# Ordering small TensorE products by tile size, and moving a block's transposes from TensorE to the DMA crossbar

## The chip, the cores and the metric

The kernel runs on one core of one Trainium2 chip. The metric is the device time of one execution in microseconds (us), median over several runs. A run counts as slow when it is over 1.5% above the fastest run of the same kernel; the medians given here for the runs use the fast runs only. The granted clock is the share of its full speed that TensorE was allowed (1.00 is full); landing is the time from a DMA's issue to the arrival of its data; a transpose on the DMA crossbar is a DMA that transposes the tile that it moves. A ratio below is the mean time of one kernel's fast runs over that of the other's in the same rounds, so it is not quite the ratio of the medians that stand beside it.

## The reference, cut to what matters

```python
# 4 batches, 8 heads, 768 steps, head size 48
for t in range(S):                      # gated linear attention
    state = alpha[:, :, t, :, None] * state + einsum('bhd,bhe->bhde', k[:, :, t], v[:, :, t])
    y[:, :, t] = einsum('bhd,bhde->bhe', q[:, :, t], state)
x = y.transpose(0, 2, 1, 3).reshape(3072, 384)
r = maximum(x @ w_in, 0.0)              # w_in 384 x 2048
out = (s * r * r + b) @ w_out           # w_out 2048 x 384
```

## The kernel before

Attention works on 24 blocks of 128 steps (6 in each of 4 sequences), all 8 heads at once. For a block, b is the running product of alpha. The block needs the transposes of q\*b and k/b (4 tiles of 128x128 each), the score products, and the y products (state times q, and v times masked scores). The y products of 8 heads of 48 columns are cut at the borders of quadrants (32 columns each), so some are 64 columns wide and some 32.

```python
def st_T(n):                            # 8 transposes on TensorE, into PSUM
    for x, src in ((0, qb_sb[n % 2]), (1, kb_sb[n % 2])):
        f = src.rearrange("a h d -> a (h d)")
        for p in range(NP):
            nc.tensor.transpose(out=t_ps[:, x, p, :], in_=f[:, 128*p : 128*p + 128], identity=ident_bf)

def st_Tcopy(n):                        # VectorE copies them to SBUF
    nc.vector.tensor_copy(out=qkT_sb[n % 2]..., in_=t_ps...)

# (pair of heads, [head,] first 32-column quadrant, width in quadrants)
S_PARTS = [(0, 0, 2), (0, 2, 1), (1, 3, 1), (1, 4, 2), (2, 6, 2), (2, 8, 1), (3, 9, 1), (3, 10, 2)]
V_PARTS = [
    (0, 0, 0, 2), (0, 1, 2, 1), (1, 0, 3, 1), (1, 1, 4, 2), (2, 0, 6, 2), (2, 1, 8, 1),
    (3, 0, 9, 1), (3, 1, 10, 2), (0, 1, 1, 1), (1, 0, 4, 1), (2, 1, 7, 1), (3, 0, 10, 1),
]
def st_y(n):
    for p, x, m in S_PARTS: ...         # state^T q, 8 products
    for p, e, x, m in V_PARTS: ...      # v^T masked scores, 12 products
```

All work goes through a small list scheduler inside the kernel: each operation is booked with an engine, an assumed duration, a priority and a latency, the scheduler simulates, and the instructions are emitted in the order of its simulated start times. Each engine then runs its own list strictly in that order.

```python
op("SP", 0.98, rank + 0.1 * x, load, n, src, dst, w=[(name, ii)], lat=2.0)
op("PE", 0.5, t + 0.3, st_T, n, r=[("qb", i2), ("kb", i2)], w=["ct"], lat=0.27)
op("DVE", 0.61, t + 0.4, st_Tcopy, n, r=["ct"], w=[("qkT", i2)])
op("PE", 0.33, t + 0.5, st_A, n, r=[("qkT", i2)], w=["a"], lat=0.27)      # scores
op("PE", 0.6, t + 0.7, st_y, n, r=rr, w=["py"], lat=0.27)
op("ACT", 0.43, t + 0.8, st_yevac, n, r=["py"], w=[("xd", ...)])
# ... and the MLP: mm1 (w_in, PE), relu (ACT), square (DVE), mm2 (w_out, PE), output
```

## Time and profile before

| | before |
|---|---|
| median | 233.87 us (3 runs, 233.66 to 234.86; the profiled run took 235.56) |
| TensorE busy | 211.7 us of 233.8 |
| TensorE idle from 52 us to its last matmul | 0 |
| y products of one block | 1.70 us |

The windows view of the kernel before gives stretches of the run: from and to, length, then the busy time of TensorE, its weight loads, VectorE, ScalarE and GpSimd, the granted clock of TensorE, the mean busy share of the 16 DMA engines and their GB/s:

```profile
30.00:40.00 10.00, 8.06 (x86) 5.64 (x84) 7.20 (x13) 3.25 (x6) 7.21 (x5) 1.00 0.95 289
40.00:52.00 12.00, 10.33 (x95) 6.53 (x92) 12.00 (x21) 5.50 (x12) 4.39 (x4) 0.86 1.01 223
52.00:75.00 23.00, 23.00 (x240) 14.95 (x238) 18.72 (x44) 12.90 (x31) 5.16 (x7) 1.00 0.77 160
75.00:100.00 25.00, 25.00 (x276) 16.59 (x276) 16.08 (x41) 11.97 (x26) 4.49 (x7) 1.00 0.88 181
100.00:125.00 25.00, 25.00 (x242) 13.75 (x242) 17.29 (x32) 12.33 (x29) 3.32 (x5) 1.00 0.85 176
```

The first busy column is TensorE: it fills every stretch from 52 us on, so there each microsecond taken off it counts. Before 52 us it does not fill them. The DMA share is 0.77 to 0.88 from 52 to 125 us.

The first four groups of weight loads of one block's y products, in the timeline of TensorE's weight loads (start, duration, engine, line, operation, operands, array tile, count):

```profile
118.63 0.11 PEld L409 LDWEIGHTS <-s_st_144 128*64 128x64 bf16 x1 [0.42 <-issue]
118.80 0.10 PEld L409 LDWEIGHTS <-s_st_144 128*32 128x32 bf16 x2
118.97 0.11 PEld L409 LDWEIGHTS <-s_st_144 128*64 128x64 bf16 x2
119.14 0.10 PEld L409 LDWEIGHTS <-s_st_144 128*32 128x32 bf16 x2
```

A change between 128\*64 and 128\*32 tiles comes every 0.17 us, with one product in the group or two; the last group, at 120.16, has four and takes 0.17 us as well. Ten groups make the 1.70 us, which the chain of waits of the same block shows as two halves (start, duration):

```profile
118.70 0.85 PE py_ps L409 x8
119.55 0.85 PE py_ps L419 x12
120.40 0.76 PE o_ps_69 L479 x4
```

### The profile page before, as it was taken

How to read it: one execution, taken by the hardware profiler on the slowest of the kernel's cores; microseconds unless marked ns; L12 is line 12 of the kernel's file. 1: busy time of each engine (PE TensorE's matmuls, PEld its weight loads, DVE VectorE, ACT ScalarE, POOL GpSimd, SP SyncE). 2: the span in 40 equal slices, each digit the busy share in tenths (PEclk: the TensorE clock that was granted, in tenths of full speed). 3: DMA queues.
4: the chain of work that ended last, by engine and by line, in shares of the span. 5: the costliest groups of instructions: out<-in, count | busy, mean ns of one | idle time of the engine just before them, and what ended most of it. 6: DMA issues, size and time to landing. Idle time of an engine off the chain costs nothing.

```text
span 233.8 us, 4929 instructions
## 1 busy us (share of the span) xinstructions
PE 211.7 (91%) x1916; PEld 123.9 (53%) x1916; DVE 144.0 (62%) x283; ACT 100.8 (43%) x217; POOL 45.4 (19%) x63
## 2 busy tenths in 40 slices
PE   0268696799999999999999999999999999999993
PEld 0134473466676666655555555545555555555562
DVE  2266459998779666675767865597656754343321
ACT  3213351554565534523656545675354433444300
POOL 5234439333102220200202120001210100000000
PEclk9999999799999999999999999999999999999999
DMA  6999798995789989689895464300000100101111
GB/s 135 184 289 249 199 366 197 242 205 111 157 171 213 192 190 185 143 172 215 170 181 101 97 146 104 67 3 34 35 3 34 36 0 34 36 35 38 64 70 67
DMA packets 107320, 30.21 MB, mean 129 GB/s; under 512 B 100640, under 2 KB 105760, under 8 KB 107296
## 3 DMA queue, kind: packets, MB, share of 16 engines
q1 hardware_dynamic: 107296, 29.89, 55.2%
q8 instruction: 15, 0.25, 0.5%
q14 instruction: 9, 0.07, 0.1%
HBM read 25.17 MB, written 4.72 MB: 128 GB/s over the span
## 4 chain that ended last, share of the span: by engine, by line
PE 82%; SPq 7%; DVE 5%; DMA 3%; issue 1%; ACT 0%
PE h_ps_67 L455 14%; PE o_ps_69 L479 14%; PE h_ps_66 L455 14%; PE o_ps_68 L479 13%; PE py_ps L419 8%; PE py_ps L409 7%; SPq L175 5%; PE ct_ps L324 4%; PE a_ps L370 3%; PE py_ps L335 3%; DMA a_in_73<-in_alpha_dram 3%; PE ct_ps L281 2%; SPq L220 1%; DVE colpart L247 1%; DVE colsum L252 1%
## 5 line engine op out<-in xcount | busy, mean ns | idle before, releaser
L464 ACT ACTIVATE r_149<-h_ps_66 128x512 bf16<-128x512 f32 x48 | 28.7, 598 | 46.2 <-PE h_ps_66 L455 37.4
L455 PEld LDWEIGHTS <-w_in_bf 128*128 128x128 bf16 x384 | 34.9, 100 | 22.0 <-issue 2.1
L464 ACT ACTIVATE r_150<-h_ps_67 128x512 bf16<-128x512 f32 x48 | 28.7, 599 | 20.1 <-PE h_ps_67 L455 13.5
L455 PE MATMUL h_ps_66<-xd_147,w_in_bf 128*128 128x512 bf16 (+1 forms) x72 | 17.0, 357 | 0.0
L379 DVE TENSOR_TENSOR am_138<-a_ps,mask 128x1024 bf16<-128x1024 f32 x12 | 14.7, 1222 | 3.4 <-PE a_ps L370 3.2
L344 DVE COPY qkT_136<-ct_ps 128x1024 bf16<-128x1024 bf16 x12 | 8.3, 688 | 13.7 <-PE ct_ps L324 13.7
L455 PE MATMUL h_ps_67<-xd_147,w_in_bf 128*128 128x512 bf16 (+1 forms) x72 | 16.5, 348 | 0.0
L344 DVE COPY qkT_137<-ct_ps 128x1024 bf16<-128x1024 bf16 x12 | 8.3, 690 | 12.9 <-PE ct_ps L324 12.8
L379 DVE TENSOR_TENSOR am_139<-a_ps,mask 128x1024 bf16<-128x1024 f32 x12 | 14.7, 1221 | 2.3 <-PE a_ps L370 2.0
L455 PE MATMUL h_ps_67<-xd_146,w_in_bf 128*128 128x256 bf16 (+1 forms) x72 | 13.8, 321 | 1.5 <-ACT r_150 L464 1.5
L455 PE MATMUL h_ps_66<-xd_146,w_in_bf 128*128 128x256 bf16 (+1 forms) x72 | 13.9, 323 | 0.0
L364 POOL TENSOR_TENSOR s_st_144<-t_142,blast_140 128x384 bf16<-128x384 bf16 x8 | 7.7, 968 | 24.6 <-DVE t_142 L356 17.7
L433 ACT ACTIVATE xd_147<-py_ps 128x384 bf16<-128x384 f32 x10 | 4.9, 490 | 15.2 <-PE py_ps L419 15.2
L409 PE MATMUL py_ps<-qkT_137,s_st_144 128*64 128x128 bf16 (+1 forms) x96 | 11.4, 242 | 0.0
L324 PE MATMUL ct_ps<-ident_bf,qb_128 128*128 128x128 bf16 x48 | 5.1, 234 | 5.4 <-DVE qb_128 L308 5.4
L409 PEld LDWEIGHTS <-s_st_144 128*64 128x64 bf16 (+1 forms) x96 | 6.2, 101 | 6.9 <-issue 3.5
L455 PE MATMUL h_ps_66<-xd_148,w_in_bf 128*128 128x256 bf16 (+1 forms) x48 | 9.8, 327 | 0.0
L455 PE MATMUL h_ps_67<-xd_148,w_in_bf 128*128 128x256 bf16 (+1 forms) x48 | 9.8, 327 | 0.0
L364 POOL TENSOR_TENSOR s_st_145<-t_143,blast_141 128x384 bf16<-128x384 bf16 x8 | 7.0, 879 | 13.3 <-DVE t_143 L356 11.2
L419 PEld LDWEIGHTS <-vp_113 128*32 128x32 bf16 (+1 forms) x96 | 5.0, 99 | 6.3 <-issue 3.5
L281 PE MATMUL ct_ps<-la_97,U_bf 128*128 128x384 bf16 x12 | 4.5, 376 | 4.1 <-ACT la_97 L275 4.1
L295 ACT ACTIVATE b_s_125<-ct_ps 128x384 f32<-128x384 f32 x12 | 5.9, 489 | 5.4 <-PE ct_ps L286 5.1
(207 smaller groups left out, 480.8 us busy)
## 6 DMA issues: line engine op xcount, KB each, us to landing
out_dram<-o_sb_167 SPq DMA_DIRECT2D x8, 192.0 KB, 2.0
out_dram<-o_sb_168 SPq DMA_DIRECT2D x8, 192.0 KB, 2.0
out_dram<-o_sb_169 SPq DMA_DIRECT2D x8, 192.0 KB, 1.9
a_in_70<-in_alpha_dram SPq DMA_DIRECT2D x5, 192.0 KB, 4.2
q_in_75<-in_q_dram SPq DMA_DIRECT2D x5, 192.0 KB, 3.6
k_in_80<-in_k_dram SPq DMA_DIRECT2D x5, 192.0 KB, 3.9
v_in_85<-in_v_dram SPq DMA_DIRECT2D x5, 192.0 KB, 4.0
a_in_71<-in_alpha_dram SPq DMA_DIRECT2D x5, 192.0 KB, 3.6
```

Of the source, the lines that this page charges most:

```text
L175: nc.sync.dma_start(out=dst[n % NIN], in_=src[b, :, c * C : (c + 1) * C, :].rearrange("h s d -> s h d"),)
L281: nc.tensor.matmul(out=cum_ps, lhsT=U_bf, rhs=la[:, :, 0:D], start=True, stop=True)
L324: nc.tensor.transpose(out=t_ps[:, x, p, :], in_=f[:, 128 * p : 128 * p + 128], identity=ident_bf,)
L335: nc.tensor.matmul(out=p_ps[64 * e : 64 * e + 64, p, :], lhsT=kb[:, 128 * p + 64 * e : 128 * p + 64 * e + 64], rhs=vp[:, p, 48 * e : 48 * ...
L344: nc.vector.tensor_copy(out=qkT_sb[n % 2].rearrange("a x p t -> a (x p t)"), in_=t_ps.rearrange("a x p t -> a (x p t)"),)
L364: nc.gpsimd.tensor_tensor(out=s_sb[n % 2], in0=t1_sb[n % 2], in1=bl, op=ALU.mult)
L379: nc.vector.tensor_tensor(out=am_sb[n % 2].rearrange("a e p t -> a (e p) t"), in0=a_ps.rearrange("a e p t -> a (e p) t"), in1=mask.unsquee ...
L409: nc.tensor.matmul(out=y_ps[r0 : r0 + 32 * m, kk, :], lhsT=st[:, p, c0 : c0 + 32 * m], rhs=qT[:, p, :], start=(x < 4), stop=False,)
L419: nc.tensor.matmul(out=y_ps[r0 : r0 + 32 * m, kk, :], lhsT=vp[:, p, c0 : c0 + 32 * m], rhs=am[:, e, p, :], start=(first and i < 3), stop=( ...
L455: nc.tensor.matmul(out=hp[:, i * n : (i + 1) * n], lhsT=w_in_bf[:, kk, 128 * j : 128 * (j + 1)], rhs=xd_sb[g % 3][:, kk, 0:n], start=(kk = ...
L464: nc.scalar.activation(out=r_sb[w % 2], in_=h_ps[w % 2], func=AF.Relu)
L479: nc.tensor.matmul(out=op[:, 0:d_model], lhsT=gt_sb[j][:, c0 : c0 + C], rhs=w_out_bf[:, j, :], start=(j == 0), stop=(j == NJ - 1),)
```

## The change

The intent is to take work off TensorE in two ways: order the y products so that the tile size changes once, and give the transposes of blocks 4 to 23 to the DMA crossbar (one DMA of 128x1024 bf16 a block, issued by ScalarE), which also frees VectorE of its copy. To make room, q\*b and k/b share one tile with three buffers, and v has four buffers. Two loads of 128 x 1 elements (s and b) move from the SP queue to GpSimd.

```diff
+NPE = 4
-    vp_sb = many("vp", 3, ...)
+    vp_sb = many("vp", 4, ...)
-    qb_sb = many("qb", 2, [128, H, 64], BF16, zero=nc.vector)
-    kb_sb = many("kb", 2, [128, H, 64], BF16, zero=nc.vector)
-    qkT_sb = many("qkT", 2, [128, 2, NP, 128], BF16)
+    qk_sb = many("qk", 3, [128, 2, H, 64], BF16, zero=nc.vector)
+    qkT_sb = many("qkT", 3, [128, 2, NP, 128], BF16)
+    def st_Tdma(n):
+        nc.scalar.dma_start_transpose(
+            out=qkT_sb[n % 3].rearrange("a x p t -> a (x p) t"),
+            in_=qk_sb[n % 3].rearrange("a x h d -> a (x h d)"),
+        )
-    S_PARTS = [...]
-    V_PARTS = [...]
+    Y_PARTS = [                                     # None: a state product
+        (0, None, 0, 2), (2, None, 6, 2), (1, None, 4, 2), (3, None, 10, 2),
+        (0, 0, 0, 2), (2, 0, 6, 2), (1, 1, 4, 2), (3, 1, 10, 2),
+        (2, None, 8, 1), (3, None, 9, 1), (0, None, 2, 1), (1, None, 3, 1),
+        (2, 1, 8, 1), (3, 0, 9, 1), (0, 1, 2, 1), (1, 0, 3, 1),
+        (1, 0, 4, 1), (0, 1, 1, 1), (3, 0, 10, 1), (2, 1, 7, 1),
+    ]
     # ... st_y runs through Y_PARTS in this order
-                op("SP", 0.5, t + 0.5, lambda: nc.sync.dma_start(out=b_col, ...
+                op("POOL", 0.5, t + 0.5, lambda: nc.gpsimd.dma_start(out=b_col, ...
     # ... the same for s_col
+            if n < NPE:
                 op("PE", 0.5, t + 0.3, st_T, n, ...)
                 op("DVE", 0.61, t + 0.4, st_Tcopy, n, ...)
+            else:
+                op("ACT", 0.3, t + 0.3, st_Tdma, n, r=[("qb", i3), ("kb", i3)],
+                   w=[("qkT", i3)], lat=3.5)
-            op("PE", 0.6, t + 0.7, st_y, ...)
+            op("PE", 0.55, t + 0.7, st_y, ...)
```

More of the change, by code (lines that the diff above doesn't have):

```diff
@@ L192 @@
     nc.vector.memset(ones_col_bf, 1.0)
-    vp_sb = many("vp", 3, [128, NP, VW], BF16, zero=nc.gpsimd)
+    vp_sb = many("vp", 4, [128, NP, VW], BF16, zero=nc.gpsimd)
     mask = sb.tile([128, 128], BF16, name="mask")
@@ L302, in st_vcast @@
         nc.gpsimd.tensor_copy(
-            out=vp_sb[n % 3].rearrange("a p (x d) -> a p x d", d=D)[:, :, 0:3:2, :],
+            out=vp_sb[n % 4].rearrange("a p (x d) -> a p x d", d=D)[:, :, 0:3:2, :],
             in_=v_in[n % NIN].rearrange("a (p e) d -> a p e d", e=2),
@@ L308, in st_qb @@
         nc.vector.tensor_tensor(
-            out=qb_sb[n % 2][:, :, 0:D], in0=q_in[n % NIN], in1=b_sb[n % 2], op=ALU.mult
+            out=qk_sb[n % 3][:, 0, :, 0:D], in0=q_in[n % NIN], in1=b_sb[n % 2], op=ALU.mult
         )
@@ L313, in st_kb @@
         nc.vector.tensor_tensor(
-            out=kb_sb[n % 2][:, :, 0:D],
+            out=qk_sb[n % 3][:, 1, :, 0:D],
             in0=k_in[n % NIN],
@@ L320, in st_T @@
     def st_T(n):
-        for x, src in ((0, qb_sb[n % 2]), (1, kb_sb[n % 2])):
-            f = src.rearrange("a h d -> a (h d)")
+        f = qk_sb[n % 3].rearrange("a x h d -> a (x h d)")
+        for x in range(2):
             for p in range(NP):
+                c0 = 512 * x + 128 * p
                 nc.tensor.transpose(
-                    out=t_ps[:, x, p, :],
-                    in_=f[:, 128 * p : 128 * p + 128],
-                    identity=ident_bf,
-                )
+                    out=t_ps[:, x, p, :], in_=f[:, c0 : c0 + 128], identity=ident_bf
+                )
+    def st_Tdma(n):
[3 more added lines that the diff above has]
+        )
     def st_KV(n):
-        kb = kb_sb[n % 2].rearrange("a h d -> a (h d)")
-        vp = vp_sb[n % 3]
+        kb = qk_sb[n % 3][:, 1].rearrange("a h d -> a (h d)")
+        vp = vp_sb[n % 4]
         for p in range(NP):
@@ L344, in st_Tcopy @@
         nc.vector.tensor_copy(
-            out=qkT_sb[n % 2].rearrange("a x p t -> a (x p t)"),
+            out=qkT_sb[n % 3].rearrange("a x p t -> a (x p t)"),
             in_=t_ps.rearrange("a x p t -> a (x p t)"),
@@ L366, in st_A @@
     def st_A(n):
-        qkT = qkT_sb[n % 2]
+        qkT = qkT_sb[n % 3]
         for p in range(NP):
@@ L384, in st_mask @@
         )
-    def quadrant(x):
-        return x // 4, 32 * (x % 4)
-    S_PARTS = [(0, 0, 2), (0, 2, 1), (1, 3, 1), (1, 4, 2), (2, 6, 2), (2, 8, 1), (3, 9, 1), (3, 10, 2)]
-    V_PARTS = [
-        (0, 0, 0, 2), (0, 1, 2, 1), (1, 0, 3, 1), (1, 1, 4, 2), (2, 0, 6, 2), (2, 1, 8, 1),
-        (3, 0, 9, 1), (3, 1, 10, 2), (0, 1, 1, 1), (1, 0, 4, 1), (2, 1, 7, 1), (3, 0, 10, 1),
+    Y_PARTS = [
[5 rows of a table added]
     ]
@@ L400, in st_y @@
         first = n % NCH == 0
-        qT = qkT_sb[n % 2][:, 0]
+        qT = qkT_sb[n % 3][:, 0]
         am = am_sb[n % 2]
-        vp = vp_sb[n % 3]
+        vp = vp_sb[n % 4]
         st = s_sb[(n - 1) % 2]
-        if not first:
-            for p, x, m in S_PARTS:
-                kk, r0 = quadrant(x)
-                c0 = 32 * x - 96 * p
-                nc.tensor.matmul(
-                    out=y_ps[r0 : r0 + 32 * m, kk, :],
-                    lhsT=st[:, p, c0 : c0 + 32 * m],
-                    rhs=qT[:, p, :],
-                    start=(x < 4),
-                    stop=False,
-                )
-        for i, (p, e, x, m) in enumerate(V_PARTS):
-            kk, r0 = quadrant(x)
-            c0 = 32 * x - 96 * p + 48 * e
-            nc.tensor.matmul(
-                out=y_ps[r0 : r0 + 32 * m, kk, :],
-                lhsT=vp[:, p, c0 : c0 + 32 * m],
-                rhs=am[:, e, p, :],
-                start=(first and i < 3),
-                stop=(i >= 8),
+        parts = [x for x in Y_PARTS if not (first and x[1] is None)]
+        fresh = {0, 1, 2, 3}
+        for i, (p, e, x, m) in enumerate(parts):
+            c0 = 32 * x - 96 * p
+            mine = {(x + y) % 4 for y in range(m)}
+            start = mine <= fresh
+            fresh -= mine
+            nc.tensor.matmul(
+                out=y_ps[32 * (x % 4) : 32 * (x % 4) + 32 * m, x // 4, :],
+                lhsT=(
+                    st[:, p, c0 : c0 + 32 * m]
+                    if e is None
+                    else vp[:, p, c0 + 48 * e : c0 + 48 * e + 32 * m]
+                ),
+                rhs=qT[:, p, :] if e is None else am[:, e, p, :],
+                start=start,
+                stop=(i >= len(parts) - 4),
             )
@@ L527 @@
                     sched.done((name, 0), 3.5 + x)
-                op("SP", 0.5, t + 0.5,
-                   lambda: nc.sync.dma_start(out=b_col, in_=moe_b.to_broadcast((128, 1))),
+                op("POOL", 0.5, t + 0.5,
+                   lambda: nc.gpsimd.dma_start(out=b_col, in_=moe_b.to_broadcast((128, 1))),
                    w=["b"], lat=2.0)
-                op("SP", 0.5, t + 0.6,
-                   lambda: nc.sync.dma_start(out=s_col, in_=moe_s.to_broadcast((128, 1))),
+                op("POOL", 0.5, t + 0.6,
+                   lambda: nc.gpsimd.dma_start(out=s_col, in_=moe_s.to_broadcast((128, 1))),
                    w=["s"], lat=2.0)
@@ L567 @@
             op("ACT", 0.55, t + 0.1, st_exp_i, n, r=["ct"], w=[("bi", i2), ("bl", i2)])
-            op("POOL", 0.6, t + 0.2, st_vcast, n, r=[("v", ii)], w=[("vp", i3)])
-            op("DVE", 0.47, t + 0.2, st_qb, n, r=[("q", ii), ("b", i2)], w=[("qb", i2)])
-            op("DVE", 0.47, t + 0.2, st_kb, n, r=[("k", ii), ("bi", i2)], w=[("kb", i2)])
-            op("PE", 0.5, t + 0.3, st_T, n, r=[("qb", i2), ("kb", i2)], w=["ct"], lat=0.27)
-            op("DVE", 0.61, t + 0.4, st_Tcopy, n, r=["ct"], w=[("qkT", i2)])
-            op("PE", 0.34, t + 0.35, st_KV, n, r=[("kb", i2), ("vp", i3)], w=["py"], lat=0.27)
+            op("POOL", 0.6, t + 0.2, st_vcast, n, r=[("v", ii)], w=[("vp", n % 4)])
+            op("DVE", 0.47, t + 0.2, st_qb, n, r=[("q", ii), ("b", i2)], w=[("qb", i3)])
+            op("DVE", 0.47, t + 0.2, st_kb, n, r=[("k", ii), ("bi", i2)], w=[("kb", i3)])
+            if n < NPE:
+                op("PE", 0.5, t + 0.3, st_T, n, r=[("qb", i3), ("kb", i3)], w=["ct"], lat=0.27)
+                op("DVE", 0.61, t + 0.4, st_Tcopy, n, r=["ct"], w=[("qkT", i3)])
+            else:
+                op("ACT", 0.3, t + 0.3, st_Tdma, n, r=[("qb", i3), ("kb", i3)],
+                   w=[("qkT", i3)], lat=3.5)
+            op("PE", 0.34, t + 0.35, st_KV, n, r=[("kb", i3), ("vp", n % 4)], w=["py"], lat=0.27)
             if first(n):
@@ L578 @@
                 op("POOL", 0.9, t + 0.1, st_snew, n, r=[("t1", i2), ("bl", i2)], w=[("S", i2)])
-            op("PE", 0.33, t + 0.5, st_A, n, r=[("qkT", i2)], w=["a"], lat=0.27)
+            op("PE", 0.33, t + 0.5, st_A, n, r=[("qkT", i3)], w=["a"], lat=0.27)
             op("DVE", 1.15, t + 0.6, st_mask, n, r=["a"], w=[("am", i2)])
-            rr = [("am", i2), ("qkT", i2), ("vp", i3)] + ([] if first(n) else [("S", 1 - i2)])
-            op("PE", 0.6, t + 0.7, st_y, n, r=rr, w=["py"], lat=0.27)
+            rr = [("am", i2), ("qkT", i3), ("vp", n % 4)] + ([] if first(n) else [("S", 1 - i2)])
+            op("PE", 0.55, t + 0.7, st_y, n, r=rr, w=["py"], lat=0.27)
             op("ACT", 0.43, t + 0.8, st_yevac, n, r=["py"], w=[("xd", g % 3, blk_group[n][1])])
```

## The prediction

> **What bounds the kernel now.** The windows view has TensorE busy 23.00 of 23, 25.00 of 25, 25.00 of 25 ... in every stretch from 52 to 197 us, and the chain of waits is 82% TensorE. Before 52 us it is starved (0.57 of the first 10 us, 6 to 8 of each later 10): there the DMA share is 0.78 to 1.01 and VectorE is full from 40 to 52 us. After 197 us only MLP matmuls remain. From 52 to 197 us VectorE (99 of 145 us) and ScalarE (73) have slack. So this middle stretch, with attention blocks 4 to 23 at 7.2 us each, is where TensorE work removed counts one for one.
>
> **y products.** In the timeline of one block (118.6 to 120.3 us), the 20 products start in groups: 118.63 (64 columns), 118.80 (32, 32), 118.97 (64, 64), 119.14, 119.31, 119.48 ... 120.33. A change between 64 and 32 columns costs 0.17 us whether one, two or four products stand in the group: 10 groups = 1.70 us. This fits the Trainium skill, "TensorEngine Tiling (Array Packing)", Key Properties: changing the tiling mode drains the array, and tiles of one mode run in parallel. The k-v products, all 64 wide, show the second half: pairs at 114.29, 114.32, 114.36, 114.41 us, so two column tiles run together (96 columns, 40 ns a pair). Reordered: 8 of 64 columns, then 12 of 32, one change. Estimate: 3 x 0.053 + 0.17 and 2 x 0.053..0.08 + 0.17 = 0.6 to 0.66 us in place of 1.70; a sequence's first block 0.44 in place of 1.02. Over blocks 4 to 23 (17 and 3): 17 x 1.06 + 3 x 0.58 = 19.8 us.
>
> **Transposes.** Eight transposes hold TensorE 0.55 us (120.83 to 121.38); 20 blocks leave them: 11.3 us. VectorE loses 20 copies of 0.69 us, 13.8 us off the critical path. Added: 20 DMA transposes of 256 KiB, issued on ScalarE. The Trainium skill, "DMA: Bandwidth & Descriptors", gives an effective 261 GB/s: estimate 1.0 to 1.3 us of all 16 engines a block, 3 to 5 us from issue to landing when shared with loads (a 192 KB load now lands in 3.6 to 4.6 us). No trace here shows one yet. DMA share is 0.77 to 0.88 from 52 to 125 us; at 5.6 us a block it comes close to 1, so loads will lose their lead and some score products will wait for their transposed operands. ScalarE issue time: 0.3 to 1.5 us a block, which can delay a ReLU. I charge 4 us in all for such waits.
>
> **Start.** The two one-column loads (0.98 and 0.59 us in the DMA queue, the first on the chain) go to GpSimd: later loads start 1.5 us earlier; up to 1 us gained. Early reorders (blocks 0 to 3) fall in starved time: about 0.
>
> **Sum.** 233.9 - 19.8 - 11.3 - 0.8 + 4 = 206 us. Range 198 to 218. Faster by over 2%: 0.96; within: 0.03; slower: 0.01.
>
> **What would show each step.** y: two groups of loads a block, TensorE y time near 0.6 us. Transposes: transposes at n<4 only, 20 ScalarE DMA issues landing in 3 to 5 us; DMA share 0.9 or more from 52 to 115 us. Pace 5.5 to 6 us a block. TensorE idle under 6 us from 52 us to the end; waits of score products on the DMA.
>
> **What would make it wrong.** Slow transposes (3 us or more of engine time a block) would make DMA the bound at about 7 us a block: 212 to 220 us. A long ScalarE hold would stall the first MLP product through ReLU. If four 32-column tiles don't run together, y stays near 0.9 us: +5 us. No stalls and a faster start: 200 us.

## The result

The changed kernel takes 217.38 us (4 runs, 216.72 to 218.90), the kernel before 234.06 us beside it: ratio 0.9293, interval 0.9236 to 0.9349. That is 16.7 us off; 27.9 us had been forecast. The time lies in the stated range, the gain is 60% of the forecast one.

The same stretches of the changed kernel's windows view:

```profile
30.00:40.00 10.00, 6.77 (x46) 3.56 (x45) 8.75 (x11) 1.27 (x4) 7.95 (x6) 0.67 1.01 283
40.00:52.00 12.00, 8.07 (x71) 5.30 (x70) 11.36 (x22) 5.76 (x13) 5.13 (x4) 0.85 0.85 180
52.00:75.00 23.00, 22.34 (x263) 14.41 (x263) 16.89 (x40) 12.50 (x31) 2.63 (x5) 1.00 1.10 201
75.00:100.00 25.00, 21.91 (x278) 14.35 (x276) 17.73 (x43) 13.88 (x34) 5.90 (x9) 1.00 1.19 205
100.00:125.00 25.00, 22.09 (x219) 11.09 (x217) 17.19 (x31) 14.85 (x34) 5.33 (x7) 1.00 1.27 209
```

TensorE now idles in the stretches that it filled, and is busy for less of the time before 52 us. The DMA share is 1.10 to 1.27. It sums the times of packets, so over 1 it says that the times of packets overlap on the engines.

The y products of one block, again in the timeline of the weight loads:

```profile
94.91 0.14 PEld L420 LDWEIGHTS <-s_st_146 128*64 128x64 bf16 x4 [0.32 <-issue]
95.00 0.17 PEld L420 LDWEIGHTS <-vp_117 128*64 128x64 bf16 x4
95.26 0.10 PEld L420 LDWEIGHTS <-s_st_146 128*32 128x32 bf16 x4
95.27 0.16 PEld L420 LDWEIGHTS <-vp_117 128*32 128x32 bf16 x8
95.54 0.11 PEld L376 LDWEIGHTS <-qkT_138 64*128 64x128 bf16 x4
```

One change of tile size, at 95.26; the whole takes 0.63 us in place of 1.70. The eight products of 64 columns, four pairs, take 0.35 us and the twelve of 32 columns, three fours, 0.28 us. If the first pair and the first four take 0.17 us each, as every group did before, a further one adds about 0.06 us; so an estimate for one change is 0.11 us. This part came out as forecast. The DMA queues of the changed kernel (packets, MB, share of the 16 engines' span; then landing times in us):

```profile
q1 hardware_dynamic: 107008, 29.89, 65.3%
q10 hardware_dynamic: 21120, 5.25, 16.0%
...
qkT_137<-qk_132 ACTq DMA_TRANSPOSE x7, 5.4
qkT_138<-qk_134 ACTq DMA_TRANSPOSE x7, 4.8
qkT_136<-qk_130 ACTq DMA_TRANSPOSE x6, 5.5
```

Queue 10 holds the transposes: 16.0% of 214.9 us over 20 transposes is 1.72 us of all 16 engines for each. The loads and stores in queue 1 moved the same bytes as before, yet took 65.3% of 214.9 = 140 us of the engines, where before they took 55.2% of 233.8 = 129 us. And TensorE waits, in its own timeline:

```profile
83.19 0.33 PE L484 MATMUL o_ps_68<-w_out_bf,gt_163 128*128 128x384 bf16 x1
84.81 0.40 PE L376 MATMUL a_ps<-qkT_136 64*128 64x128 bf16 x8 [1.30 <-DMA qkT_136<-qk_130]
85.66 0.60 PE L460 MATMUL h_ps_67<-xd_147,w_in_bf 128*128 128x256 bf16 x4 [0.46 <-ACT r_151 L469]
```

The last line waits for ScalarE, but ScalarE itself was late because a load was. Its timeline has, just before that ReLU:

```profile
84.60 0.52 ACT L276 ACTIVATE la_97<-a_in_72 128x384 bf16<-128x384 f32 x1 [2.61 <-DMA a_in_72<-in_alpha_dram]
```

Adding up such gaps from the trace, from 52 us on: 4.9 us before score products and 2.3 us before first MLP products, 7.2 us where there had been none. Over the whole run the pages give TensorE's busy time as 211.7 and 181.7 us, so 30.0 us less, but its idle time is 233.8 - 211.7 = 22.1 and 214.9 - 181.7 = 33.2 us, 11.1 us more. Of these 11.1 us, 7.2 lie after 52 us and most of the rest before it. A second profile of the same kernel (e11 below) has 3.7 and 1.9 us of such gaps, and 5.7 us of idle time in all from 52 us to the last matmul; so the loss after 52 us is 5.7 to 7.2 us.

### The profile page after: what moved, and what is told of

Its sections match the earlier page's. It is cut to its first block, busy times and chain, and to the rows that moved or that the text cites. A ratio compares the mean times of both kernels' runs of the same rounds, so it can differ in the third digit from the quotient of the medians.

```text
span 214.9 us, 4590 instructions
## 1 busy us (share of the span) xinstructions
PE 181.7 (85%) x1756; PEld 103.6 (48%) x1756; DVE 138.6 (64%) x262; ACT 98.5 (46%) x217; POOL 49.2 (23%) x66
## 3 DMA queue, kind: packets, MB, share of 16 engines
q1 hardware_dynamic: 107008, 29.89, 65.3%
## 4 chain that ended last, share of the span: by engine, by line
PE 55%; DMA 19%; SPq 11%; DVE 9%; issue 3%; ACT 1%; ACTq 0%; DVEq 0%
PE o_ps_69 L484 12%; PE h_ps_67 L460 11%; PE o_ps_68 L484 11%; PE h_ps_66 L460 10%; SPq L177 9%; DMA qkT_137<-qk_132 5%; PE py_ps L420 4%; DMA wst_173<-in_moe_w_out_dram 3%; DMA qkT_136<-qk_130 3%; DMA qkT_138<-qk_134 3%; PE a_ps L376 3%; DMA a_in_72<-in_alpha_dram 3%; DMA a_in_74<-in_alpha_dram 2%; PE py_ps L341 2%; SPq L221 2%
## 5 line engine op out<-in xcount | busy, mean ns | idle before, releaser
L460 PEld LDWEIGHTS <-w_in_bf 128*128 128x128 bf16 x384 | 36.2, 101 | 29.5 <-issue 7.4
L460 PE MATMUL h_ps_66<-xd_147,w_in_bf 128*128 128x256 bf16 (+1 forms) x72 | 14.3, 332 | 0.6 <-ACT r_150 L469 0.6
L460 PE MATMUL h_ps_67<-xd_147,w_in_bf 128*128 128x256 bf16 (+1 forms) x72 | 14.2, 330 | 0.7 <-ACT r_151 L469 0.6
L370 POOL TENSOR_TENSOR s_st_145<-t_143,blast_141 128x384 bf16<-128x384 bf16 x8 | 8.9, 1107 | 18.8 <-DVE t_143 L362 14.2
L370 POOL TENSOR_TENSOR s_st_146<-t_144,blast_142 128x384 bf16<-128x384 bf16 x8 | 8.0, 995 | 14.4 <-DVE t_144 L362 13.3
L460 PE MATMUL h_ps_67<-xd_149,w_in_bf 128*128 128x256 bf16 (+1 forms) x48 | 9.8, 327 | 0.0
L460 PE MATMUL h_ps_66<-xd_149,w_in_bf 128*128 128x256 bf16 (+1 forms) x48 | 9.8, 326 | 0.0
L296 ACT ACTIVATE b_s_127<-ct_ps 128x384 f32<-128x384 f32 x12 | 5.9, 489 | 6.3 <-PE ct_ps L287 5.7
L296 ACT ACTIVATE b_s_126<-ct_ps 128x384 f32<-128x384 f32 x12 | 5.9, 490 | 4.7 <-PE ct_ps L287 4.5
L287 PEld LDWEIGHTS <-la_97 128*128 128x128 bf16 x48 | 3.1, 100 | 8.4 <-issue 7.4
L477 DVE TENSOR_TENSOR gt_152<-r_150 128x256 bf16<-128x256 bf16 (+1 forms) x8 | 2.8, 356 | 6.0 <-ACT r_150 L469 6.0
L376 PE MATMUL a_ps<-qkT_136 64*128 64x128 bf16 x64 | 3.6, 240 | 3.6 <-DMA qkT_136<-qk_130 3.5
L299 ACT ACTIVATE binv_129<-ct_ps 128x384 f32<-128x384 f32 x12 | 5.9, 493 | 0.9 <-DVE qk_132 L309 0.9
L484 PE MATMUL o_ps_68<-w_out_bf,gt_152 128*128 128x384 bf16 x12 | 4.1, 339 | 2.6 <-POOL w_out_bf L241 2.6
```

The source lines that it names most:

```text
L296: nc.scalar.activation(out=b_sb[n % 2], in_=cum_ps, func=AF.Exp)
L299: nc.scalar.activation(out=binv_sb[n % 2], in_=cum_ps, func=AF.Exp, scale=-1.0)
L370: nc.gpsimd.tensor_tensor(out=s_sb[n % 2], in0=t1_sb[n % 2], in1=bl, op=ALU.mult)
L376: nc.tensor.matmul(out=a_ps[:, e, p, :], lhsT=qkT[64 * e : 64 * e + 64, 1, p, :], rhs=qkT[64 * e : 64 * e + 64, 0, p, :], start=True, stop ...
L460: nc.tensor.matmul(out=hp[:, i * n : (i + 1) * n], lhsT=w_in_bf[:, kk, 128 * j : 128 * (j + 1)], rhs=xd_sb[g % 3][:, kk, 0:n], start=(kk = ...
L484: nc.tensor.matmul(out=op[:, 0:d_model], lhsT=gt_sb[j][:, c0 : c0 + C], rhs=w_out_bf[:, j, :], start=(j == 0), stop=(j == NJ - 1),)
```

## The experiments

Theory A: the crossbar transposes give back about what they free, since they share the DMA engines with the loads. Rival B: at the new pace something else bounds, whoever transposes. A second question came up on the way: what was lost before 52 us. The record marks every kernel as correct, even e6, which loads too little. From the reference and its inputs, all of the output but the term b @ w_out is 0.4% of the output's norm, so this check says little of the attention part in any of the kernels.

| run | what | median us | ratio to before |
|---|---|---|---|
| changed kernel; again as e11 | all | 217.38; 216.33 (217.36 with two slow runs) | 0.9293; 0.9230 |
| e1 | y order alone | 214.03 | 0.9130 |
| e2 | all but the y order | 229.54 | 0.9799 |
| e3 | all but the DMA transposes | 217.61 | 0.9296 |
| e4 | DMA transposes from block 16 on | 215.64 | 0.9199 |
| e5, e9 | small loads back on SP | 214.29 (215.92 with two slow runs), 214.36 | 0.9161, 0.9166 |
| e12 | order of e9, small loads on GpSimd | 215.34 | 0.9202 |
| e6 | light loads (wrong result) | 210.86 | 0.9024 |
| e7 | scheduler told the true DMA cost | 219.80 | 0.9401 |
| e8 | e5 + e7, transposes from block 16 on | 211.49 | 0.9040 |
| e10 | as e8, from block 12 on | 210.73 | 0.8994 |

### e1: the y order alone

```diff
 # the kernel before, with Y_PARTS and its loop in place of S_PARTS and V_PARTS
-            op("PE", 0.6, t + 0.7, st_y, ...   # kept at 0.6, so that the order stays
```

> The kernel before with the reordered y products alone; the order of all engines as before. Theory A (the crossbar transposes give back about what they free: the time was lost to waits for them and to the loads they slow): TensorE loses about 23 us of y time (19.8 after 52 us) and stays without idle time after 52 us, so 211 to 214 us, faster than the changed kernel (217.4). Rival B (at this pace another engine or the loads bound, whoever transposes): TensorE idles 5 us or more after 52 us here too, 217 to 222 us.

214.03 us, ratio 0.9130. This one reordering beats the whole change. Its windows view:

```profile
52.00:75.00 23.00, 23.00 (x293) 15.38 (x292) 19.42 (x48) 13.24 (x31) 3.59 (x6) 1.00 0.85 176
75.00:100.00 25.00, 25.00 (x312) 16.31 (x311) 18.96 (x42) 12.50 (x29) 4.35 (x7) 1.00 0.99 210
100.00:125.00 25.00, 25.00 (x266) 13.09 (x264) 21.07 (x39) 16.32 (x36) 4.94 (x7) 1.00 0.86 171
```

At the faster pace TensorE still fills every stretch, so no other engine binds, and the loads keep up, with the DMA share up to 0.99. B falls. Note that 0.99: transposes added from 75 to 100 us would meet DMA engines that are already busy.

### e2 and e3: the DMA transposes without the y order, and the rest without the DMA transposes

```diff
 # e2: the changed kernel with S_PARTS, V_PARTS and their loops
 # e3: the changed kernel
-NPE = 4
+NPE = 24
```

> The changed kernel with the y products in their old order and nothing else undone. Theory A: at the slow pace of 7 us a block the transposes have more time, but each still holds ScalarE and the DMA engines: TensorE frees 9 us, 3 to 6 us come back as waits, 2 us at the start: 229 to 233 us. Rival B (transposes are fine, the pace is the limit): 224 to 226 us, no waits for the DMA.

> The changed kernel with every block transposed on TensorE (no DMA transposes), its other parts kept: 4 and 3 buffers, the two small loads on GpSimd, the y order. Theory A: as e1, 211 to 215 us; a difference of 2 us or more to e1 would be due to the small loads, the buffers and the order of the first 50 us. Rival B: 217 us or more.

e2 is 229.54 us: without the y order the rest of the change is worth 2% (1.4 to 2.6, so the verdict is unclear), more than nothing and half of what its TensorE time would give. In its trace the waits after 52 us are gone (0.06 us of idle up to the last matmul): at 7 us a block the transposes land in time. So what it lost does not lie there. The time fell into A's range, but by luck: the forecast for A, 3 to 6 us of waits, was wrong for this pace, and no waits is what B had said. Its DMA share is 1.15 to 1.21 from 52 to 125 us, about as high as in the changed kernel. So a high share alone did not make TensorE wait; in the changed kernel, where only the y order and with it the pace differ, it waited.

e3 is 217.61 us, the same as the changed kernel, though all transposes run on TensorE. So in the changed kernel the DMA transposes are worth between 0 and 1.5 us (ratio 0.9296 against 0.9293 and 0.9230, each known to about 1.3 us). By its time alone e3 fell where B had put it. And e3 differs from e1 by 3.6 us though both have the y order and all transposes on TensorE: something else in the change costs time. In its trace TensorE's idle time after 52 us is only 0.2 us, but 3.3 us more TensorE work is left to do at 52 us than in e1; so B stays out, and this loss lies before 52 us.

### e4: transposes by DMA only late

```diff
-NPE = 4
+NPE = 16
```

> The changed kernel with crossbar transposes from the 17th block on, where fewer loads run. Theory A with contention as the cause: the 8 blocks free 8 x 0.46 = 3.7 us without waits: 3 us below e3. If the wait is in the transposes themselves and not in contention: equal to e3 or above it.

215.64 us, 2.0 us under e3, with 1.1 us of idle time after 52 us and a median landing of 4.1 us. The sign is as A with contention has it, the size about half of the 3.7 us freed; the intervals of the two ratios just touch (0.9142 to 0.9256, and 0.9242 to 0.9350).

### e6: the same instructions with a quarter of the load traffic

```diff
     def load(n, src, dst):
+        nh = 2 if n >= 8 else H
         nc.sync.dma_start(
-            out=dst[n % NIN],
-            in_=src[b, :, c * C : (c + 1) * C, :].rearrange("h s d -> s h d"),
+            out=dst[n % NIN][:, 0:nh, :],
+            in_=src[b, 0:nh, c * C : (c + 1) * C, :].rearrange("h s d -> s h d"),
         )
```

> Wrong result on purpose: the changed kernel, but the loads of q, k, v and alpha from the ninth block on fetch 2 of 8 heads (the rest of the tile keeps an older block's data), so load traffic falls to a quarter while all instructions and their order stay. Theory C (transposes are late because they share the 16 DMA engines with the loads): landing falls from about 5.3 to about 3 us, the 4.9 us of waits of score products on the DMA fall under 1 us, 211 to 213 us. Rival S (the transposes are slow by themselves, or ScalarE's issue time costs the time): landing stays at 4.5 us or more, waits stay, 216 to 217 us.

210.86 us, 6.5 us under the changed kernel by the medians, 4.8 to 6.3 us by the ratios. In the trace, waits after 52 us fall from 4.9 to 0.4 us before score products and from 2.3 to under 0.1 us before first MLP products, which accounts for the gain. The windows and the landing:

```profile
75.00:100.00 25.00, 25.00 (x310) 16.14 (x309) 19.89 (x45) 15.59 (x37) 5.89 (x8) 1.00 0.69 122
100.00:125.00 25.00, 24.70 (x252) 12.71 (x251) 20.74 (x36) 16.29 (x38) 5.94 (x8) 1.00 0.55 114
...
qkT<-qk ACTq DMA_TRANSPOSE x20, 3.5
```

The transposes land in 3.5 us, what the kernel's scheduler had assumed. ScalarE still spends 1.25 us on each issue in the median, as in the changed kernel (where the longest took 2.03 us, here 1.39), so that hold alone is not what cost the time. Contention is the cause of the waits after 52 us. The run does not separate loads that delay transposes from transposes that delay loads, as both get lighter; the queue shares and the late load at 84.60 above say that both happen.

### e7: tell the scheduler the measured cost

```diff
-                op("ACT", 0.3, t + 0.3, st_Tdma, n, ..., lat=3.5)
+                op("ACT", 1.3, t + 0.3, st_Tdma, n, ..., lat=5.5)
```

> The changed kernel with its scheduler told the measured cost of a transpose: 1.3 us of ScalarE in place of 0.3 and 5.5 us to landing in place of 3.5, so that score products come later in TensorE's order. Theory W (the loss is in the order: scores are placed before their operands can land): the waits of score products fall from 4.9 to under 2 us, 213 to 215 us. Rival: the chain of one block gets longer and other waits (first MLP products on y, loads held back) take their place: 216 to 218 us.

219.80 us, worse than even the rival's range: theory W falls. The waits of score products are gone (0.01 us), but 7.9 us of idle after 52 us stay, under other names. The largest one, in the timelines of ScalarE and TensorE:

```profile
104.94 0.52 ACT L276 ACTIVATE la<-a_in 128x384 bf16<-128x384 f32 x1 [3.91 <-DMA a_in<-in_alpha_dram]
106.32 0.49 ACT L438 ACTIVATE xd<-py_ps 128x384 bf16<-128x384 f32 x1 [0.85 <-issue]
106.86 0.40 PE L341 MATMUL py_ps<-vp,qk 128*64 128x96 bf16 x5 [5.12 <-ACT xd L438]
```

ScalarE waits 3.91 us for a late load of alpha, then it issues the next transpose for 1.25 us (at 105.02); the evacuation of y stands behind both in ScalarE's list, and TensorE waits for that. So here an order that spared one wait found another. What made e7 slower than the changed kernel is not explained in full: its idle time after 52 us is only 0.7 us longer, and its granted clock from 40 to 52 us was 0.68, there 0.85.

### e5, e9 and e12: what was lost before 52 us

In the changed kernel TensorE's timeline around block 3's score products (the line at 37.26) reads:

```profile
33.59 0.48 PE L484 MATMUL o_ps_68<-w_out_bf,gt_152 128*128 128x384 bf16 x1 [2.55 <-POOL w_out_bf L241]
...
35.20 0.50 PE L484 MATMUL o_ps_68<-w_out_bf,gt_155 128*128 128x384 bf16 x1 [0.50 <-DVE gt_155 L477]
35.89 1.44 PE L460 MATMUL h_ps_67<-xd_147,w_in_bf 128*128 128x256 bf16 x6 [0.18 <-ACT r_151 L469]
37.26 0.50 PE L376 MATMUL a_ps<-qkT_136 64*128 64x128 bf16 x6
```

In the kernel before, the same scores come first, at 35.84, and the first w_out products after them:

```profile
35.84 0.40 PE L370 MATMUL a_ps<-qkT_137 64*128 64x128 bf16 x8
36.56 0.32 PE L479 MATMUL o_ps_68<-w_out_bf,gt_151 128*128 128x384 bf16 x1 [0.32 <-POOL w_out_bf L240]
```

The order has turned round. The scheduler, which no longer books the two small loads on SP, believes that the weights come earlier and puts w_out products ahead of the scores; they then wait 2.55 us for GpSimd's cast. The squares that they need are late as well: in VectorE's timeline the same operation takes 1.55 us while GpSimd casts w_out (the first line, from GpSimd's timeline), 0.28 us right after. The kernel before has such squares too (1.55 us at 36.58), but there the scores are done by then.

```profile
33.48 1.52 POOL L241 CAST w_out_bf<-wst_174 128x1536 bf16<-128x1536 f32 x1
33.60 1.55 DVE L477 TENSOR_TENSOR gt_155<-r_151 128x256 bf16<-128x256 bf16 x1
35.07 0.28 DVE L477 TENSOR_TENSOR gt_156<-r_150 128x256 bf16<-128x256 bf16 x1
```

This agrees with the Trainium skill, "SBUF — State Buffer", SBUF: two separate sides, which says of the port pair that VectorE and GpSimd share that a VectorE operation with two SBUF inputs and a GpSimd operation that reads SBUF block each other fully.

The granted clock from 30 to 40 us was 0.67, where before it was 1.00 (windows above): in windows of 1 us it is 0.50 from 34 to 38 us, and six w_in products took 1.44 us at 35.89 but 0.81 us at 40.54. In e3 and e11, where TensorE waits 1.78 and 2.88 us for the same cast, it was 0.86 and 0.79; in e1, e9 and e12, where that wait is 0.22 us or nothing, 1.00. So the lower clock came together with the wait, and how much of the loss is wait and how much is clock no run separates.

```diff
 # e5, e9: the changed kernel
-                op("POOL", 0.5, t + 0.5, lambda: nc.gpsimd.dma_start(out=b_col, ...
+                op("SP", 0.5, t + 0.5, lambda: nc.sync.dma_start(out=b_col, ...
 # the same for s_col. e12: op("SP", ...), but still nc.gpsimd.dma_start
```

> The changed kernel with the two small loads back on the SP queue, nothing else undone. Theory P (3.6 us lie between e1 and e3 because the kernel's own scheduler, believing that weights come earlier, now puts the first w_out products, the log of block 1 and the first squares ahead of block 3's attention work): the old order of the first 45 us returns, block 3's score products start near 34 us in place of 37.3, and the time falls by 2.5 to 4 us, to 213.5 to 215. Rival (the buffers or the GpSimd load itself cost it, not the order; or the transposes do): 217 us and block 3's scores still after 36 us.

> The kernel of e5 again, whose profile and one timed run fell in the slow state. Theory P (order of the first 45 us): 213.5 to 215 us in fast runs, 2.5 to 3.5 us under the changed kernel run beside it; block 3's scores near 34 us; waits of score products on the DMA still 3 us or more after 52 us, as the transposes are unchanged. Rival: within 1 us of the changed kernel.

> The changed kernel itself, as the measure for the other runs of this call: 217 us, first score products of block 3 near 37 us.

> The changed kernel with the small loads still issued by GpSimd, but booked on SP in the kernel's own scheduler, so that all engines get the order of e5 (TensorE's order was compared and is the same). Theory P (the order costs the 3 us, not the place of the loads): 213.5 to 215 us as e5, block 3's scores near 34 us. Rival (the load on GpSimd itself, or the earlier SP loads, cost it): 217 us, block 3's scores at 37 us or later.

In e5 the profiled run and one timed run were slow; its two fast runs took 215.33 and 213.25 us. Run again as e9 (six fast runs, 213.83 to 216.81) it gave 214.36 us. The changed kernel itself beside it (e11) gave 216.33 us over its four fast runs; by the ratios the difference is 1.5 us, less than theory P's 2.5 to 3.5, and the intervals, 0.9117 to 0.9216 and 0.9175 to 0.9286, overlap. Against the first measure of the changed kernel (0.9293) it is 3 us. So a gain of 1.5 to 3 us is likely and not shown. What the profiles show is the start: the scores of block 3 come at 39.0 us in e11 and at 34.70 us in e9, where the w_out products follow them:

```profile
34.70 0.40 PE L376 MATMUL a_ps<-qkT 64*128 64x128 bf16 x8 [0.18 <-DVE qkT L350]
35.03 0.82 PE L484 MATMUL o_ps<-w_out_bf,gt 128*128 128x384 bf16 x4
```

e12 asks whether it is the order or the place of the loads: TensorE's order was compared with e9's and is the same, and only the queue of the two loads differs. The scores of block 3 come at 32.9 us, so the order brings the start back. The granted clock from 30 to 40 us is 1.00 again. Its time, 215.34 us, varied from 212.50 to 215.58 and its ratio (0.9146 to 0.9257) fits either side. That the order moved the start is shown; what it is worth in time, and whether the place of the loads has a small cost of its own, stays open. So does the part of the 3.6 us between e3 and e1 that the other buffers may have: no run changed them alone.

With the start mended, e9 (0.9166, DMA transposes) and e1 (0.9130, none) are level: once more the DMA transposes from block 4 on are worth nothing that the runs resolve, and e9 still idles 6.2 us after 52 us.

### e8 and e10: putting it together

```diff
 # e5 with e7's costs and
-NPE = 4
+NPE = 16     # e10: 12
```

> Attempt at a faster kernel: y order, small loads on SP, crossbar transposes from the 17th block on, the scheduler told 1.3 and 5.5 us. If the causes add up: e1 less 8 transposes of TensorE (3.7 us) plus under 1 us of waits: 210.5 to 212 us. If the transposes cost what they free also here: 214 us.

> The kernel of e8 with crossbar transposes from the 13th block on in place of the 17th: four more blocks, 1.9 us less on TensorE, while loads still fill the DMA engines. Theory C: these four come back as waits or late loads, so within 1 us of e8 (211.5), more likely above. Rival: 209.5 to 210 us.

e8 takes 211.49 us with 0.3 us of idle after 52 us, e10 210.73 us with 2.36 us, ratio 0.8994 (0.8953 to 0.9034). The two are level within their intervals. Both beat the changed kernel by about 6 us and e1 by 2 to 3 us. They differ from e1 in buffers and bookings too, but in the profiles e8 has 3.7 us less TensorE work after 52 us than e1, which is what its eight blocks free. e10's four further blocks bring about 0.8 us of the 1.9 us that they free, within the noise; its windows show waits, as TensorE loses 2.1 us just as the transposes begin (the first is issued at 99.4 us):

```profile
100.00:125.00 25.00, 22.90 (x218) 11.35 (x217) 19.91 (x35) 16.55 (x39) 4.52 (x6) 1.00 1.07 197
125.00:150.00 25.00, 25.00 (x250) 13.08 (x249) 17.97 (x32) 15.54 (x34) 4.17 (x6) 1.00 0.78 144
```

## Why the prediction was right or wrong

- **What bounds: right.** TensorE, from 52 us on. e1 confirms it, filling every stretch at the faster pace.
- **y products, -19.8 us: right.** From the trace, start to next work: 31.97 us in the 20 blocks after 52 us before, 12.19 us in the changed kernel (two waits, 1.2 us in all, taken off), 19.8 us less. e1 alone took about 20 us off the time. That four 32-column tiles run together held: 12 products from 95.26 to 95.54.
- **Transposes off TensorE, -11.3 us: too large.** I took 0.55 us from one block. By start to next work, 152 transposes after 52 us took 8.87 us, 0.47 us a block, so 9.3 us for 20.
- **"I charge 4 us in all for such waits": this step failed.** The mechanism was named (share close to 1, late loads, scores waiting), the size was not: 7.2 us after 52 us, 5.7 in the second profile. e6 shows that sharing the DMA engines with the loads is the cause. The estimate of 1.0 to 1.3 us of the engines from the skill's 261 GB/s was low; by its packets' time a transpose has 1.72 us in the trace, and the loads' own packets took 11 us more in all. Against that the transposes free 9.3 us on TensorE, so with the waits little is left: nothing to 1.5 us by e3.
- **Start, -0.8 us: wrong in sign.** With the small loads gone from SP, block 1's alpha was issued at 3.48 us in place of 5.11, but the block 3 scores came 1.4 us later, and e3 against e1 puts the loss, the buffers' part included, at 3.6 us. That makes this step's miss, 4.4 us, larger than that of the waits, 3.2, and of the transposes, 2.0. I priced the loads and overlooked that the kernel's scheduler reorders all engines when a booking changes.
- **The total.** The 217.38 us lie close to the edge of 198 to 218. The gain rests on the y products, whose step was right; the other steps together lost about 3 us (e1 took 214.03). The time also lies in the 212 to 220 us that were given for transposes of 3 us or more of engine time, which was not what happened (1.72 us), so the number alone says little of the steps.
- **Signs in the profile.** A DMA share of 0.9 or more and waits of scores on the DMA came. Landing in 3 to 5 us came out as 4.8 to 5.5. Idle under 6 us held in one of two profiles (5.7 and 7.2). The pace of 5.5 to 6 us a block did not come: score products of blocks 4 to 23 run from 52.56 to 177.62 us, 6.6 us a block, and 6.5 in e1.

## What to carry to other kernels

Order small matmuls by tile size: a group of one to four products took 0.17 us here when its size was new, and about 0.06 us when it was not, and this order alone gained more than the whole change. Before work moves to the DMA engines, read their share in the very stretch it moves to, at the pace that it will have: at 0.85 to 0.99 (e1) the transposes gave back what they freed; from the 13th or 17th block on, closer to the end of the loads, e10 and e8 came out 2 to 3 us under e1. With blocks 7 us apart (e2) they caused no waits at all. In a kernel that is emitted from an internal schedule, compare each engine's order of before and after first, as a change of one booking can move work far from the thing booked: here the start of block 3's scores by 1.4 to 4.3 us.

## What the Trainium skill lacked or had wrong

- "TensorEngine Tiling (Array Packing)", Key Properties, says that a change of tiling mode drains the array, but not what it costs: 0.17 us from one group to the next here, with one, two or four products in the group, of which about 0.11 us is an estimate for the change.
- "DMA: Bandwidth & Descriptors", Latency and other measured facts, gives 261 GB/s for transposes with a non-contiguous middle dimension, measured on one kernel, and more for contiguous ones. By the time of its packets, a transpose of 128x1024 bf16 from SBUF to SBUF (262,144 bytes) took 1.72 us of the 16 engines beside the loads, 152 GB/s, and 1.55 us (14.9% of 208.2 us over 20) with light loads, 169 GB/s. No run has a transpose without loads, so this is no measure of one alone.
- The same page, Rules for kernel authors, says that a transpose next to ordinary DMAs needs nothing. It speaks of correctness there; in time it landed in 4.8 to 5.5 us beside full loads, 3.5 us beside light ones.
- No page gives the issue time on trn2 of a transpose of this shape: ScalarE's queue is held 1.25 us for each in the median, and up to 2.03 us.
- "TensorE: Matmul & The Clock Gate", PE-mode transpose, gives about 275 ns for a transpose in a kernel, as the length of one. Eight in a row here cost 58 ns each from start to start (8.87 us over 152), which is the number to plan with when they follow each other.
